# Batch 0's state softmax with tokens on partitions, in a fused cross-attention and PReLU MLP kernel on one core

## The chip, the cores and the metric

The kernel runs on one core of a Trainium2 chip. The metric is the time of one execution on the device, in microseconds (us). The engines are named as the profile names them: PE is TensorE (matrix products), PEld its weight load, DVE is VectorE, ACT is ScalarE, POOL is GpSimd and SP is SyncE. SBUF is the on-chip memory that the engines work in. PSUM is the memory into which PE writes: eight banks, each of 512 f32 values on each of 128 partitions.

## What is computed

Eight batches (B) of eight heads (H), each with 512 tokens (S) and 32 states (N) of width 64 (D). The 32 states of each head attend to the tokens and the tokens to the states; both reads are put side by side, and every row (4,352 of width 512) goes through an MLP with one hidden layer of 2,048 units and a PReLU with a slope for each unit.

```python
scores = scale * x @ state.T              # per batch and head: 512 x 32
a      = softmax(scores, over the 32 states)
xread  = a @ state
a2     = softmax(scale * state @ x.T, over the 512 tokens)
sread  = a2 @ x
rows   = concatenate([xread, sread], axis=2)    # 544 rows of 512 a batch
h   = rows @ w_in                          # 512 -> 2048
g   = maximum(h, 0) + alpha * minimum(h, 0)
out = g @ w_out                            # 2048 -> 512
```

## The kernel before

**The work.** For the token rows the kernel never makes xread. It multiplies the states of a batch by w_in first: `m = state @ w_in` (step `m.b.f`, L458, one for each batch and each quarter f of w_in, that is 512 hidden units; `mo`, L480, casts it to f16 into SBUF, in two halves of four heads). The first layer is then `h = a.T x m` (step `F.b.jc`, L491, for one of 16 blocks jc of 128 hidden units): two matmuls of 512 columns over the whole array, one for each half g of the heads. In batch 0 some of them are cut into their halves as steps `f.b.jc.g` (L512). Then ACT computes relu(-h) (step `N`, L523), DVE the PReLU from that and h (step `G`, L531), PE the second layer (step `S.b.q.jc2`, L543: two blocks jc for a quarter q of the tokens, over the whole array, 512 columns each), and `O` copies the result out of PSUM (L581) and issues its store. The state rows of all batches are a ninth batch at the end: `F.8` (L500), `R` (L591) and `RO`. The last quarter of the last batch is done in three pieces (`L`, L563, and `LO`, L574).

**Batch 0's way to its weights.** x is cast to f16 by its load (`lx0`, two halves by heads), turned by PE (`xt`, L288) and copied to SBUF (`xo`, L293; `xo2`, L296, is the same for batch 1). The states go the same way: `stc`, `stt`, `sto` for batch 0, whose load comes first; `str` (L234) and `sro` (L265, two copies of 896 columns) for the rest, whose load `lst` comes after the first x. Scores are computed by PE with the states on partitions (`sc`, L308: 64x32 tiles, eight for each half of the heads). The token softmax works on them as they are: `tm` (the maximum, L389, scaled at L392), `te` (exp with its sum, ACT, L400), `tsum` (L410), `tn` (POOL, L414), `tt` (a transposing DMA). The state softmax wants the 32 states of a token side by side. So DVE turns the scores in 32x32 blocks (`sb`, L343 for one half, L341 for a whole batch), takes the maximum over 32 columns (`smax`, L349), POOL subtracts it (`ssh.p`, L355), ACT takes exp (`sexp`, L361), DVE sums and inverts (`ssum`, L365 and L366), POOL scales to f16 (`snorm.p`, L369), and DVE turns the weights back in 32x32 blocks (`wb`, L377). Batch 0 does this in two halves of the heads, the later batches in one.

**What sets the order.** `ORDER` (L17 to L102) lists every step in the sequence in which each engine gets its instructions; nothing reorders them. A step's last arguments are its PSUM bank (k0 to k5) where it takes one, or its engine: a for ACT, v for DVE, p for POOL. A seventh tile of two banks, `two`, holds scores, or an `m` without a bank of its own. Each of these has one buffer, so the next user of a bank waits until the one before has been read. `Z.k.n` gives PE n x 128 columns of zeros to multiply (L218), to fill time in which nothing else is ready. The load of x of a batch (`lx`), of w_in by quarters (`wi`) and of w_out (`wo`) cast from f32 to f16 and are issued by POOL, in its instruction order, and run through one queue: `lx0.0 lx0.1 lst wi.0 lx.1 wi.1 wo.0 wi.2 wo.1 wi.3 wo.2 lx.2 wo.3`, then the other batches' x. From batch 2 on, x is turned by a DMA that SP issues (`xd`).

**Matmul shapes.** `sc` and `m` use 64x32 tiles of PE's array (the profile writes 64*32), the state reads `rd` (L433) 128*64; `xt`, `F`, `f`, `S` use the whole array (128*128). "Tiled" below means the former.

Of the kernel before, what the change touches and what calls it, by code (L numbers as in the profile page):

```python
# [34 lines left out]
S.0.0.7 S.0.3.6 N.1.1 G.1.1 N.1.3 tn.1.0 O.0.0.a te.2.0 F.1.5.4 S.0.3.7 N.1.5 G.1.3 F.1.9.2
S.1.1.0.5 G.1.7 F.1.4.3 smax.2 O.0.3.a S.1.1.1 tn.1.1 G.1.5 rd.0.0 te.2.1 N.1.9 G.1.9 m.2.3 F.1.6.1
N.1.4 rdo.0.a F.1.12.4 N.1.6 lx.3 G.1.4 F.1.13.0 N.1.12 F.1.8.2 G.1.6 G.1.12 S.1.2.0.3 N.1.13 G.1.13
ssh.p.2 N.1.8 S.1.1.2 F.1.11.1 G.1.8 F.1.10.4 N.1.11 S.1.2.1 N.1.10 G.1.11 G.1.10 S.1.2.2 sexp.2
S.1.1.3 ssum.2 F.1.14.0 F.1.15.2 snorm.p.2 mo.2.3.a.0 S.1.1.4 mo.2.3.a.1 S.1.1.5 m.3.2 m.4.2.1.4
N.1.14 tt.1 tsum.2 N.1.15 G.1.14 mo.3.2.a.1 S.1.1.6 S.1.2.3 S.1.2.4 mo.3.2.a.0 mo.4.2.a.0 G.1.15  # L40
# [612 lines left out]
```

## Time and profile before

| | us |
|---|---|
| median of 3 runs | 218.55 |
| lowest and highest run | 218.24, 218.85 |
| the profiled execution | 218.35 |
| its span, first to last instruction | 216.6 |
| PE busy in the span | 209.9 |
| DVE, ACT, POOL busy | 166.5, 137.2, 71.1 |

The profile is of one execution. A line of a group reads: source line, engine, operation, output <- inputs, tile of the array (rows*columns) where PE has one, output and input shapes (partitions x elements, type), count, then after the bar the busy time of all and the mean of one in ns, then the engine's idle time just before them and who ended it. A line of one instruction reads: start and length in us, engine, line, operation, and in brackets the wait before it and who ended it. "x8" behind such a line means that eight like it are put together, and the length covers them all. L12 is line 12 of the kernel.

### The profile page before, as it was taken

What the parts mean: (1) busy time and instruction counts of PE and PEld (TensorE: products, weight loads), DVE (VectorE), ACT (ScalarE), POOL (GpSimd) and SP (SyncE); (2) the same over time, 40 slices, a digit from 0 to 9 for tenths busy, and PEclk for the clock granted to TensorE, in tenths of its full rate; (3) what the DMA queues carried; (4) which work ended last, traced back from release to release, by engine and by line L of the source; (5) the groups of instructions that cost most, each with busy time, mean ns of one, the idle gap of its engine ahead of it and who ended that gap; (6) DMA issues with size and microseconds to landing.
All of it is one profiled execution on the core that took longest, in us unless ns stands there. A gap on an engine that the chain in (4) does not pass through costs nothing.

```text
span 216.6 us, 4193 instructions
## 1 busy us (share of the span) xinstructions
PE 209.9 (97%) x1637; PEld 99.9 (46%) x1637; DVE 166.5 (77%) x253; ACT 137.2 (63%) x271; POOL 71.1 (33%) x58
## 2 busy tenths in 40 slices
...
GB/s 89 174 196 206 207 199 183 127 206 127 59 137 145 81 213 98 51 108 195 174 109 97 100 50 49 2 97 48 53 147 24 28 48 48 48 47 4 48 100 145
DMA packets 39716, 23.12 MB, mean 107 GB/s; under 512 B 22144, under 2 KB 35984, under 8 KB 39696
## 3 DMA queue, kind: packets, MB, share of 16 engines
...
q14 instruction: 7, 0.06, 0.1%
...
## 4 chain that ended last, share of the span: by engine, by line
PE 90%; DMA 5%; POOL 2%; issue 1%; DVE 1%; ACT 0%; POOLq 0%
PE o L543 50%; PE h L491 25%; DMA w_in_sb<-in_moe_w_in_dram 5%; PE m_ps L458 4%; PE h L500 3%; PE o L591 3%; PE o L563 2%; PE sr_ps L433 2%; PE sc L308 1%; DVE m L480 1%; POOL xg L179 1%; POOL xg L162 0%; PE h L512 0%; POOL w_in_sb L198 0%; ACT m L480 0%
## 5 line engine op out<-in xcount | busy, mean ns | idle before, releaser
L543 PE MATMUL o<-w_out_sb,gt 128*128 128x512 f16 x496 | 125.3, 379 | 0.0
L523 ACT ACTIVATE neg<-h 128x512 f32<-128x512 f32 (+1 forms) x144 | 77.1, 579 | 46.8 <-PE h L491 37.4
L531 DVE SCALAR_TENSOR_TENSOR gt<-neg,oma_sb,h 128x512 f16<-128x512 f32 x128 | 89.9, 738 | 15.5 <-ACT neg L523 14.5
L543 PEld LDWEIGHTS <-gt 128*128 128x128 f16 x496 | 47.3, 98 | 55.3 <-issue 3.4
L491 PE MATMUL h<-aT,m 128*128 128x512 f16 x250 | 68.3, 379 | 0.0
L491 PEld LDWEIGHTS <-m 128*128 128x128 f16 x250 | 24.1, 98 | 28.3 <-issue 0.6
L414 POOL TENSOR_SCALAR e<-e,r 128x512 f16<-128x512 f16 x16 | 25.0, 1566 | 20.5 <-DVE r L410 16.6
L480 ACT CAST m<-m_ps 128x512 f16<-128x512 f32 x50 | 27.2, 611 | 4.5 <-PE m_ps L458 4.2
L369 POOL TENSOR_TENSOR an<-ts,r 128x1024 f16<-128x1024 f32 (+1 forms) x9 | 15.5, 1720 | 33.9 <-DVE r L366 14.8
L355 POOL TENSOR_TENSOR ts<-ts,mx 128x1024 f32<-128x1024 f32 (+1 forms) x9 | 15.5, 1721 | 28.7 <-DVE mx L349 28.7
L581 ACT COPY osb<-o 128x512 f32<-128x512 f32 x22 | 12.9, 591 | 14.9 <-PE o L543 14.9
L458 PE MATMUL m_ps<-w_in_sb,stT 64*32 64x512 f16 x256 | 11.4, 383 | 0.5 <-DMA w_in_sb<-in_moe_w_in_dram 0.4
L400 ACT ACTIVATE e<-sc,nb 128x512 f16<-128x512 f32 x16 | 11.2, 705 | 1.1 <-DVE nb L392 1.1
L377 DVE STREAM_TRANSPOSE aT<-an 128x1024 f16<-128x1024 f16 (+1 forms) x9 | 10.1, 1121 | 2.1 <-POOL an L369 2.1
L531 DVE SCALAR_TENSOR_TENSOR gs<-neg,oma_sb,h 128x256 f16<-128x256 f32 x16 | 7.5, 478 | 4.5 <-ACT neg L523 4.5
L480 DVE CAST m<-m_ps 128x512 f16<-128x512 f32 x14 | 9.1, 679 | 1.9 <-ACT m L480 1.6
L389 DVE TENSOR_REDUCE nb<-sc 128x2 f32<-128x1024 f32 x8 | 9.6, 1204 | 0.3 <-PE sc L308 0.3
L349 DVE TENSOR_REDUCE mx<-ts 128x32 f32<-128x1024 f32 (+1 forms) x9 | 9.8, 1091 | 0.0
L365 DVE TENSOR_REDUCE r<-ts 128x32 f32<-128x1024 f32 (+1 forms) x9 | 9.8, 1088 | 0.0
L500 PE MATMUL h<-XS,w_in_sb 128*128 128x256 f16 x64 | 9.4, 273 | 0.0
L601 DVE COPY osr<-o 128x512 f32<-128x512 f32 x1 | 0.7, 691 | 11.3 <-PE o L591 11.3
L361 ACT ACTIVATE ts<-ts 128x1024 f32<-128x1024 f32 (+1 forms) x9 | 8.7, 967 | 0.2 <-POOL ts L355 0.2
...
## 6 DMA issues: line engine op xcount, KB each, us to landing
...
```

The costliest lines, as they stand in the source:

```text
L355: engine(e).tensor_tensor(ts, ts, over_blocks(cols(live["mx", b], j, S // N)), ALU.subtract)
L369: engine(e).tensor_tensor(blocks(cols(live["an", b], j, S)), blocks(cols(live["ts", b], j, S)), over_blocks(cols(live["r1", b], j, S // N) ...
L400: nc.scalar.activation(live["e2", b][:, g, :, :], live["sc", b][:, :, :, g, :].rearrange("p r j s -> p (r j) s"), EXP, bias=live["nb", b][ ...
L414: nc.gpsimd.tensor_scalar_mul(e2, e2, live["r2", b][:, g : g + 1])
L458: nc.tensor.matmul(t[N * k : N * (k + 1), :], st_head(b, h)[64 * r : 64 * r + 64, :], w_in_sb[64 * r : 64 * r + 64, c, 512 * f : 512 * (f ...
L480: copier(e)(m_tile(b)[:, f, g, :], live["mp", b, f][g])
L491: nc.tensor.matmul(h.rearrange("p (r j s) -> p r j s", r=2, j=2), ms[b][:, f, g, 128 * j : 128 * (j + 1)], weights(b, g), start=(g == 0), ...
L500: nc.tensor.matmul(h, w_in_sb[:, c, 128 * jc : 128 * (jc + 1)], XS[:, c].rearrange("p q n b -> p (q n b)"), start=(c == 0), stop=(c == n_c ...
L523: nc.scalar.activation(neg, h, RELU, bias=0.0, scale=-1.0)
L531: nc.vector.scalar_tensor_tensor(gt, negs.pop((b, jc)), oma_sb[:, jc : jc + 1], h, ALU.mult, ALU.add)
L543: nc.tensor.matmul(outs[b, q], gts[b, jc][:, 128 * q : 128 * (q + 1)], w_out_sb[:, jc, :], start=(jc == 0), stop=(jc == n_jc - 1),)
L581: copier(e)(osb, t)
```

## The change

Batch 0's state softmax takes its scores in another form. The two halves g of the heads stay.

- `bdo.r` (`first_states_spread`) copies batch 0's states out of PSUM into `spread`, a zeroed tile in which each head has a 128 x 64 matrix: the head's states stand twice, once for the upper 64 rows and once for the lower. So `sto` leaves the PSUM tile alive.
- `tb.j.g` (`token_blocks`) multiplies turned x (128 tokens as weights) by that matrix: four whole-array matmuls of 64 columns, whose result has tokens on partitions and the 32 states of each token side by side. Both j of a half fill one bank.
- `bmax.g` takes the maximum and `bsh.g` subtracts it, on DVE, both straight from PSUM. They replace `sb.0`, `smax.0` and `ssh.p.0`.
- `sexp`, `ssum` and `snorm.p` are as before.
- `bt.g` (`first_weights_transposed`) turns the f16 weights back by four PE transposes into a bank, and `bto.g` copies them to SBUF. They replace `wb.0`.
- The scores with states on partitions are still computed once for the token softmax, as one `sc.0` instead of two halves.
- `zero` and a zero matmul's widest form are 384 columns instead of 512. The buffer `e2` has three copies instead of two.
- `ORDER` is new from end to end: sequence, banks and engines of the copies. `sro.0` and `xo` swap engines, for example, and batch 4's shift is `ssh.v.4` (DVE) where it was `ssh.p.4` (POOL). No other function is touched, and the steps of the other batches are the same list, in another sequence and with other banks and engines of copies.

```diff
 ORDER = """
-stc lx0.0 lx0.1 oma id Z.1.24 stt.0 Z.2.13 xt.0.0.0.1 sto.a xt.0.1.0.2 xo.0.0.0.v lst xo.0.1.0.v
-Z.0.6 sc.0.0 xt.0.1.1.3 xt.0.0.1.4 sb.0.0 xo.0.0.1.v smax.0.0 xo.0.1.1.a str.0.5 sc.0.1 str.1.0 wi.0
-sro.0.a lx.1 wi.1 ssh.p.0.0 sb.0.1 Z.1.3 sc.0 Z.5.7 m.0.0.1.2 sro.1.a sexp.0.0 smax.0.1 m.3.0.3.4
-ssh.p.0.1 tm.0 mo.0.0.a.1 sexp.0.1 ssum.0.0 m.1.0.5.0 ssum.0.1 te.0.1 te.0.0 mo.1.0.v.1 wo.0
-mo.1.0.a.0 snorm.p.0.0 mo.3.0.a.1 Z.2.23 xt.1.1.1.2 xt.1.0.1.2 xt.1.1.0.0 xt.1.0.0.0 mo.0.0.a.0
-snorm.p.0.1 wb.0.0 mo.3.0.a.0 m.2.0 f.0.0.0.5 f.0.1.0.4 wi.2 mo.2.0.a.0 wb.0.1 mo.2.0.a.1 f.0.1.1
-xo2.1.0.v N.0.1 m.0.1.1.3 f.0.0.1 mo.0.1.a.1 m.1.1 N.0.0 xo2.1.1.v mo.0.1.v.0 f.0.2.0.0 F.0.3.2
-f.0.2.1 F.0.4.1 mo.1.1.v.0 mo.1.1.a.1 F.0.7.3 G.0.1 N.0.2 G.0.0 wo.1 F.0.5.4 N.0.3 G.0.2 wi.3 m.4.0
-N.0.4 S.0.0.0.5 N.0.5 G.0.3 tsum.0 S.0.1.0.0 N.0.7 mo.4.0.a.1 G.0.4 S.0.0.1 S.0.1.1 G.0.5 mo.4.0.a.0
-tn.0.1 m.0.2.2.1 sc.1 G.0.7 S.0.2.0.4 mo.0.2.a.0 tm.1 m.1.2.2.3 wo.2 tn.0.0 mo.0.2.a.1 mo.1.2.a.0
-S.0.2.1 lx.2 wo.3 sb.1 F.0.6.1 F.0.9.2 mo.1.2.a.1 N.0.6 S.0.2.2 S.0.0.2 N.0.9 G.0.6 S.0.1.2 smax.1
-te.1.1 te.1.0 F.0.11.3 G.0.9 ssh.p.1 F.0.8.1 N.0.8 N.0.11 S.0.0.3 S.0.1.3 m.0.3 G.0.8 F.0.10.2
-mo.0.3.a.0 N.0.10 sexp.1 S.0.2.3 mo.0.3.v.1 xd.2 G.0.11 G.0.10 S.0.3.0.1 m.1.3 S.0.3.1 mo.1.3.a.0
-F.0.14.3 S.0.2.4 F.0.13.2 N.0.14 tt.0 ssum.1 S.0.0.4 S.0.1.4 S.0.0.5 S.0.3.2 G.0.14 F.0.12.3 N.0.13
-G.0.13 F.0.15.2 snorm.p.1 N.0.12 N.0.15 mo.1.3.a.1 wb.1 S.0.3.3 S.0.1.5 S.0.3.4 G.0.12 S.0.2.5
-G.0.15 S.0.3.5 F.1.2.3 S.0.2.6 N.1.2 F.1.0.2 tsum.1 S.0.2.7 N.1.0 S.0.1.6 S.0.1.7 G.1.2 O.0.2.a sc.2
...
-F.3.2.0 te.4.0 S.2.3.1 S.2.3.2 N.3.6 N.3.2 F.3.13.1 S.2.0.4 te.4.1 ssh.p.4 N.3.13 G.3.3 G.3.6
...
+stc lx0.0 lx0.1 id Z.1.24 stt.0 sto.a Z.2.13 xt.0.0.0.1 bdo.0.v oma xo.0.0.0.a xt.0.1.0.2 xo.0.1.0.a
+Z.5.9 xt.0.0.1.3 xt.0.1.1.4 lst xo.0.1.1.v bdo.1.a Z.1.4 tb.0.0.5 wi.0 xo.0.0.1.a tb.1.0.5 bmax.0
+tb.0.1.1 tb.1.1.1 bmax.1 str.1.2 bsh.0 str.0.0 lx.1 bsh.1 wi.1 Z.3.20 m.0.0.4.3 sro.1.a sro.0.v
+sexp.0.0 sc.0 sexp.0.1 mo.0.0.a.1 wo.0 m.3.0.5.2 ssum.0.0 mo.3.0.a.1 m.1.0.1.0 snorm.p.0.0
+mo.1.0.a.0 Z.3.10 m.4.0.3.2 mo.4.0.a.1 mo.0.0.a.0 mo.3.0.a.0 ssum.0.1 Z.1.10 bt.0.1 snorm.p.0.1
+Z.2.3 xt.1.1.1.2 xt.1.1.0.4 xt.1.0.0.4 mo.1.0.a.1 tm.0 bto.0.v mo.4.0.v.0 xt.1.0.1.2 te.0.0 bt.1.5
+f.0.2.0.1 bto.1.v f.0.0.0.0 f.0.1.0.3 xo2.1.0.v f.0.1.1 f.0.0.1 xo2.1.1.v m.0.1.5.4 te.0.1
+mo.0.1.v.1 f.0.2.1 N.0.1 N.0.0 mo.0.1.a.0 F.0.3.2 wi.2 G.0.1 G.0.0 m.1.1.4.5 N.0.2 G.0.2 mo.1.1.a.0
+m.2.0 F.0.4.3 N.0.3 mo.2.0.a.1 G.0.3 F.0.6.4 S.0.0.0.0 F.0.5.1 N.0.6 N.0.4 G.0.6 N.0.5 wo.1
+mo.2.0.a.0 S.0.2.0.2 mo.1.1.a.1 G.0.4 S.0.0.1 wi.3 S.0.2.1 m.0.2.4.3 mo.0.2.a.0 sc.1 G.0.5
+mo.0.2.a.1 tsum.0 sb.1 S.0.1.0.5 m.1.2.1.4 S.0.1.1 mo.1.2.a.1 F.0.7.3 tm.1 F.0.9.4 mo.1.2.a.0 N.0.7
+F.0.8.1 S.0.2.2 N.0.9 G.0.7 smax.1 G.0.9 te.1.1 te.1.0 N.0.8 S.0.0.2 F.0.11.3 N.0.11 wo.2 S.0.2.3
+S.0.1.2 lx.2 m.0.3 wo.3 G.0.8 F.0.10.4 tn.0.0 G.0.11 mo.0.3.a.1 S.0.0.3 ssh.p.1 S.0.1.3 mo.0.3.a.0
+N.0.10 F.0.14.1 m.1.3 sexp.1 F.0.12.3 G.0.10 S.0.2.4 ssum.1 S.0.0.4 S.0.1.4 S.0.2.5 F.0.13.4 N.0.12
+G.0.12 N.0.14 N.0.13 tn.0.1 S.0.0.5 G.0.14 S.0.3.0.3 tsum.1 S.0.3.1 snorm.p.1 F.0.15.1 S.0.1.5
+N.0.15 G.0.13 wb.1 G.0.15 S.0.3.2 S.0.3.3 xd.2 F.1.2.4 S.0.0.6 N.1.2 S.0.0.7 F.1.0.1 mo.1.3.a.1
+mo.1.3.a.0 tt.0 tn.1.1 S.0.1.6 G.1.2 O.0.0.v tn.1.0 S.0.2.6 N.1.0 G.1.0 m.2.1.4.0 sc.2 S.0.2.7
...
+G.3.8 ssh.v.4 F.3.9.5 G.3.7 N.3.4 N.3.9 F.3.0.2 sexp.4 S.2.0.5 S.2.3.0.3 G.3.4 S.2.0.6 tt.2 G.3.9
...
 """
@@ -207,18 +207,21 @@
         )
 
 
-    zero = consts.tile([128, 512], F16)
+    zero = consts.tile([128, 384], F16)
     nc.vector.memset(zero, 0.0)
 
     def zeros(k, n):
-        t = single(k, f"z_{len(zs)}", [128, 512], F32)
+        t = single(k, f"z_{len(zs)}", [128, 384], F32)
         zs.append(t)
         while n:
-            w = 128 * min(n, 4)
+            w = 128 * min(n, 3)
             nc.tensor.matmul(t[:, :w], zero[:, :128], zero[:, :w], start=True, stop=True)
             n -= w // 128
 
     zs = []
+
+    spread = consts.tile([128, H, 2, N], F16)
+    nc.vector.memset(spread, 0.0)
 
     oma_sb = consts.tile([128, n_jc], F32)
 
@@ -245,7 +248,7 @@
             twice_transposed(t[:, g, :], live["st0"][:, g, :])
 
     def first_states_out(e):
-        copier(e)(stT[:, :n0], live.pop("st0_ps").rearrange("d g p -> d (g p)"))
+        copier(e)(stT[:, :n0], live["st0_ps"].rearrange("d g p -> d (g p)"))
 
     def one_less_alpha():
         alT = consts.tile([128, 32], F32)
@@ -328,6 +331,60 @@
     def cols(t, j, n):
         return t if j is None else t[:, n * j : n * (j + 1)]
 
+    def first_states_spread(r, e):
+        d = slice(64 * r, 64 * r + 64)
+        copier(e)(
+            spread[d, :, r, :], live["st0_ps"][d].rearrange("d g (h n) -> d (g h) n", n=N)
+        )
+
+    def token_blocks(j, g, k):
+        if ("tp", g) not in live:
+            live["tp", g] = single(k, f"tp_{g}", [128, 2, 2, 4, N], F32)
+        for k in range(4):
+            h = 4 * g + (k ^ g)
+            nc.tensor.matmul(
+                live["tp", g][:, j, :, k, :],
+                live["xT", 0][:, h, j, :],
+                spread[:, h],
+                start=True,
+                stop=True,
+                skip_group_check=True,
+            )
+
+    def first_max(g):
+        if g == 0 or ("ts", 0) not in live:
+            halved.add(0)
+            live["ts", 0] = att.tile([128, 2 * S], F32, name="ts_0", tag="ts", bufs=2)
+            live["mx", 0] = att.tile([128, 2 * S // N], F32, name="mx_0", tag="mx", bufs=2)
+            live["r1", 0] = att.tile([128, 2 * S // N], F32, name="r1_0", tag="r1", bufs=2)
+            live["an", 0] = att.tile([128, 2 * S], F16, name="an_0", tag="an", bufs=2)
+            live["aT", 0] = att.tile([128, 2 * S], F16, name="aT_0", tag="aT", bufs=2)
+        nc.vector.tensor_reduce(
+            cols(live["mx", 0], g, S // N),
+            live["tp", g].rearrange("p j r k n -> p (j r k) n"),
+            AX.X, ALU.max,
+        )
+
+    def first_shift(g):
+        nc.vector.tensor_tensor(
+            blocks(cols(live["ts", 0], g, S)),
+            live.pop(("tp", g)).rearrange("p j r k n -> p (j r k) n"),
+            over_blocks(cols(live["mx", 0], g, S // N)),
+            ALU.subtract,
+        )
+
+    def first_weights_transposed(g, k):
+        t = live["wT", g] = single(k, f"wT_{g}", [128, 2, 2, 128], F16)
+        for j in range(2):
+            for r in range(2):
+                c = S * g + 256 * j + 128 * r
+                nc.tensor.transpose(t[:, r, j, :], live["an", 0][:, c : c + 128], ident)
+
+    def first_weights_out(g, e):
+        copier(e)(
+            cols(live["aT", 0], g, S), live.pop(("wT", g)).rearrange("p r j s -> p (r j s)")
+        )
+
     def score_blocks(b, j=None):
         if j in (None, 0):
             halved.discard(b) if j is None else halved.add(b)
@@ -394,7 +451,7 @@
     def token_exp(b, g):
         if ("e2", b) not in live:
             live["e2", b] = att.tile(
-                [128, 2, n_q, 128], F16, name=f"e2_{b}", tag="e2", bufs=2
+                [128, 2, n_q, 128], F16, name=f"e2_{b}", tag="e2", bufs=3
             )
             live["r2", b] = att.tile([128, 2], F32, name=f"r2_{b}", tag="r2", bufs=2)
         nc.scalar.activation(
@@ -607,7 +664,9 @@
         "lst": load_states, "wi": load_w_in, "wo": load_w_out, "lx": load_x,
         "stc": first_states_cast, "stt": first_states_transposed, "sto": first_states_out,
         "oma": one_less_alpha, "str": states_transposed, "sro": states_out,
-        "xd": x_transposed_dma, "xt": x_transposed, "xo": x_out, "xo2": x_out_both, "sc": scores,
+        "xd": x_transposed_dma, "xt": x_transposed, "xo": x_out, "xo2": x_out_both,
+        "bdo": first_states_spread, "tb": token_blocks, "bmax": first_max, "bsh": first_shift,
+        "bt": first_weights_transposed, "bto": first_weights_out, "sc": scores,
         "sb": score_blocks, "smax": state_max, "ssh": state_shift, "sexp": state_exp,
         "ssum": state_sum, "snorm": state_norm, "wb": weights_back,
         "tm": token_max, "te": token_exp, "tsum": token_sum, "tn": token_norm,
```

133 lines of the change are left out of this document (66 added, 67 removed).

## The prediction

> **What bounds the kernel now.** I read the page first, then the windows, then the chain in order of time. On the page TensorE (PE) is busy for 97% of the span and carries 90% of the chain; its matmuls overlap, so busy time alone doesn't prove that it is full.
>
> ```profile
> span 216.6 us, 4193 instructions
> PE 209.9 (97%) x1637; PEld 99.9 (46%) x1637; DVE 166.5 (77%) x253; ACT 137.2 (63%) x271; POOL 71.1 (33%) x58
> ...
> PE 90%; DMA 5%; POOL 2%; issue 1%; DVE 1%; ACT 0%; POOLq 0%
> ```
>
> The windows (length, then busy time of PE, PEld, DVE, ACT, POOL, then clock, DMA share and GB/s) say where PE is not full.
>
> ```profile
> 0.00:17.16 17.16, 13.81 (x153) 6.67 (x153) 11.20 (x26) 9.90 (x19) 11.75 (x20) 1.00 1.05 156
> 17.16:30.00 12.84, 12.75 (x110) 4.95 (x110) 12.22 (x19) 12.02 (x26) 8.19 (x7) 1.00 1.26 204
> 30.00:90.00 60.00, 59.83 (x531) 27.19 (x530) 55.22 (x78) 47.84 (x95) 23.61 (x15) 1.00 0.73 137
> 90.00:213.60 123.60, 123.56 (x848) 61.05 (x846) 87.91 (x133) 67.21 (x135) 27.56 (x17) 1.00 0.32 74
> ```
>
> From 17.16 us on PE misses 0.09, 0.17 and 0.04 us: it is full. Only the first 17.16 us, and how much work is left after them, can change. The chain (start, length) says what ends them, and gives the pace of a whole-array matmul of 512 columns, 2.16 / 10 = 0.216 us:
>
> ```profile
> 5.68 11.44 DMA w_in_sb<-in_moe_w_in_dram
> ...
> 84.84 2.16 PE o L543 x10
> ```
>
> The first row is the second quarter of w_in, issued at 5.68 and landed at 17.12. Step m.0.1 needs it, and hidden units 512 to 1023 need m.0.1. I call this **the gate**. PE just ahead of it and behind:
>
> ```profile
> 15.94 0.86 PE L512 MATMUL h<-aT,m 128*128 128x512 f16 x3
> 17.16 0.41 PE L458 MATMUL m_ps<-w_in_sb,stT 64*32 64x512 f16 x8 [0.36 <-DMA w_in_sb<-in_moe_w_in_dram]
> 17.50 0.39 PE L512 MATMUL h<-aT,m 128*128 128x512 f16 x1
> ```
>
> Three half first-layer products (step f) run from 15.94, then PE stands before the gate. The change cannot move the gate: its load has the same place in POOL's queue, behind the same five loads. It can only put more work ahead of it, and it must not delay what follows.
>
> **The state softmax, old and new.** Groups of the first 20 us (after the bar: busy us, mean ns of one), and two single rows:
>
> ```profile
> L355 POOL TENSOR_TENSOR ts<-ts,mx 128x512 f32<-128x512 f32 x2 | 2.1, 1050 | 3.8 <-DVE mx L349 3.8
> L265 ACT COPY stT<-st_ps 128x896 f16<-128x896 f16 x2 | 2.1, 1122 | 1.0 <-PE st_ps L234 1.0
> L369 POOL TENSOR_TENSOR an<-ts,r 128x512 f16<-128x512 f32 x2 | 2.1, 1039 | 0.5 <-DVE r L366 0.5
> L480 DVE CAST m<-m_ps 128x512 f16<-128x512 f32 x3 | 2.0, 671 | 0.1
> L343 DVE STREAM_TRANSPOSE ts<-sc 128x512 f32<-128x512 f32 x2 | 1.4, 718 | 0.9 <-PE sc L308 0.9
> L349 DVE TENSOR_REDUCE mx<-ts 128x16 f32<-128x512 f32 x2 | 1.4, 676 | 0.0
> L365 DVE TENSOR_REDUCE r<-ts 128x16 f32<-128x512 f32 x2 | 1.3, 654 | 0.0
> L296 DVE COPY xT<-xT_ps 128x1024 f16<-128x1024 f16 x2 | 1.2, 664 | 0.0
> L293 DVE COPY xT<-xT_ps 128x512 f16<-128x512 f16 x3 | 1.2, 412 | 2.3 <-PE xT_ps L288 2.3
> L389 DVE TENSOR_REDUCE nb<-sc 128x2 f32<-128x1024 f32 x1 | 1.2, 1215 | 0.0
> L366 DVE RECIPROCAL r<-r 128x16 f32<-128x16 f32 x2 | 0.5, 253 | 0.1
> ```
> ```profile
> 8.28 0.39 DVE L293 COPY xT<-xT_ps 128x512 f16<-128x512 f16 x1
> ...
> 14.13 1.32 PE L288 MATMUL xT_ps<-ident,xg 128*128 128x128 f16 x16
> ...
> 15.66 0.71 DVE L377 STREAM_TRANSPOSE aT<-an 128x512 f16<-128x512 f16 x1 [0.26 <-POOL an L369]
> ```
>
> Removed: four block transposes, 2 x 0.72 + 2 x 0.71 = 2.86 us of VectorE (DVE); both shifts on GpSimd (POOL), 2 x 1.05; sixteen small score matmuls. Added on PE, none of it in this trace: 16 score matmuls of 64 columns and 8 transposes of weights. The nearest row is the transposes of x, 16 in 1.32, so 24 take 2.0 us, between half of that (half the columns) and twice. They stand where zero matmuls fill time anyway, so PE pays nothing; the path pays some 0.3 us for each group. Added on DVE: two shifts out of PSUM (0.65, a reduction, to 1.05, POOL's; I take 0.70), a copy of 896 state columns from ACT (0.66 to 1.12; I take 1.0, as it reads strided, like ACT's), two copies of turned weights (0.41). ACT trades that copy (1.12) for two x copies and half a spread copy, under 0.6 each: +0.7 at most, under the 7.3 us that it idles in the first window. POOL's loads behind the gate are issued sooner, but the DMA share there is over 1, so none lands sooner. Batch 4's shift goes from POOL to DVE, with over 20 us between its scores and their use.
>
> Is it done before the gate? No scores stand ahead of the second x transposes now, and DVE does one x copy instead of three, so the copies are over by 8.2 us (8.67 before) and the first scores stand in PSUM at 8.4. From there DVE runs without a hole: two maxima 1.35, two shifts 1.40, state copy 1.00, two sums and reciprocals 1.81, token maximum and scaling 1.38, weights half 0 0.41, a cast 0.67, half 1 0.41: 8.43 us, to 16.8. In a full queue instructions overlap:
>
> ```profile
> 18.91 2.71 DVE L531 SCALAR_TENSOR_TENSOR gt<-neg,oma_sb,h 128x512 f16<-128x512 f32 x4
> 21.54 0.16 DVE L410 RECIPROCAL r<-r 128x2 f32<-128x2 f32 x1
> 21.61 0.73 DVE L531 SCALAR_TENSOR_TENSOR gt<-neg,oma_sb,h 128x512 f16<-128x512 f32 x1
> ```
>
> Four take 2.71 and one 0.73, so one per 0.66; with 0.06 saved by each of twelve it is 16.1. POOL's norms (1.04 each, from 13.1 at the latest) end by 15.2, off this path. The old half 1 was there at 15.66 + 0.71 = 16.37: **the state softmax itself gains next to nothing**. The old path waited for its engines in turn; the new one waits for DVE.
>
> **What it is worth.** The old order has three f steps behind m.0.1 (f.0.0.1 and both of jc 2), the new one has one. The two moved ahead fit into PE's hole before 17.12 and leave the full stretch: -0.43. Counting the orders, changes between tiled and whole-array matmuls behind m.0.1 fall from 41 to 40. One costs 0.10: m.0.1 takes 17.16 to 17.50 = 0.34, but three m steps in a row, the last matmul 0.39 long, pass at (0.86 - 0.39) / 2 = 0.235.
>
> ```profile
> 11.42 0.86 PE L458 MATMUL m_ps<-w_in_sb,stT 64*32 64x512 f16 x24
> ```
>
> All else behind m.0.1 is the same list in another sequence. So -0.53 if no wait changes.
>
> **New waits**, PSUM bank by bank behind the gate. PE: m.0.1 to 17.50, f and F.0.3 to 18.15, change to 18.25. There m.1.1 wants bank 4, which holds half of m.0.1 (done 17.57) until DVE's cast ends at 18.3: +0.08. m.1.1, m.2.0 and a change end at 18.9; F.0.4 wants bank 3, free after prelu G.0.1, 18.25 + 0.73 = 18.98: +0.1. F.0.4, F.0.6, S.0.0.0, F.0.5 take PE to 20.73; S.0.2.0 wants bank 2, free after the fourth prelu at 18.25 + 2.71 = 20.96: +0.23. All of PE is queued behind them; nothing makes it up. Together +0.41, and I add 0.15 for batch 1's weights, whose way from scores to use shrinks from 14.1 to 13.2 us of PE work. **Old waits** that may go:
>
> ```profile
> 22.59 0.41 PE L458 MATMUL m_ps<-w_in_sb,stT 64*32 64x512 f16 x8
> 23.09 0.41 PE L308 MATMUL sc<-xT,stT 64*32 64x256 f16 x16
> ...
> 88.83 0.40 PE L308 MATMUL sc<-xT,stT 64*32 64x256 f16 x16
> 89.37 0.41 PE L458 MATMUL m_ps<-w_in_sb,stT 64*32 64x512 f16 x8
> ```
>
> 0.50 instead of 0.235 ahead of batch 1's scores: 0.26 lost, which the new order doesn't repeat (m.2.0, whose bank they want, is cast earlier). 0.54 instead of about 0.24 at 88.83: 0.3, which may come back elsewhere. Sum: -0.53 + 0.41 + 0.15 - 0.26 = **-0.2**. The tail ends in the same last copy and store. The profiled execution took 218.35 (span 216.6 and 1.75 around it), so 218.1 by it; the median is 218.55, so I forecast 218.3. About 0.3% (0.65 us) is what a measurement can tell from no change.
>
> **Rivals.**
> *Waits vanish.* Both old waits go and the new ones don't come (shifts at 0.65, prelus from 17.9): 218.55 - 0.53 - 0.56 + 0.1 = 217.6. For it: the old order lost almost nothing after 17.16. Against: the three bank waits are written into the new one. 0.18.
> *DVE late at the gate.* Shifts at 1.05, copy at 1.12 and no overlap: half 1 at 17.6, m.0.1 half a microsecond late, and the change doesn't do what it says, as other DVE work fills the place of the block transposes: 218.8. For it: the sum above has 0.3 to spare. 0.11.
> *Banks too tight (slower).*
>
> ```profile
> L523 ACT ACTIVATE neg<-h 128x512 f32<-128x512 f32 (+1 forms) x144 | 77.1, 579 | 46.8 <-PE h L491 37.4
> ...
> L491 PE MATMUL h<-aT,m 128*128 128x512 f16 x250 | 68.3, 379 | 0.0
> ```
>
> A bank is free again 0.16 (379 less 216) + 0.58 + 0.73 us after its first-layer product, with three handings-over of some 0.05: 1.6. The old order returns to such a bank within 2 us four times, the new one thirteen times, mostly after 1.73. It decides where a prelu starts over 0.1 late. About one DVE instruction in three is one of 1.2 us, so four of thirteen might meet one, by 0.6 each: 2.4 us in a blind order, none in the old one's four; I take 1.0: 219.3. For it: DVE is busy 55.2 of 60. 0.27.
> *Half clock.* The same matmul, twice:
>
> ```profile
> 1.31 2.74 PE L218 MATMUL z<-zero 128*128 128x512 f16 x6 [1.31 <-DVE zero L211]
> ...
> 12.61 1.40 PE L218 MATMUL z<-zero 128*128 128x512 f16 x6 [0.34 <-ACT m L480]
> ```
>
> Six in 2.74, then six in 1.40; the granted clock reads 1.00 in both, so only the spacing tells. Between 14.1 and 17.1 the new PE does 24 transposes, five f and few zeros. If that slowed it again for the length of the start (1.3 to 6.6), half of 5.3 us is lost: 218.3 + 2.6 = 220.9. Against: 16 transposes and three f stood there before, at full pace. 0.04. The Trainium skill, "TensorE: Matmul & The Clock Gate", Part 4, says that transposes don't count as work for the gate that halves the clock, and Part 1 that an idle window of about 3.4 us closes it; this rival is what that rule would do. The full pace behind the 16 transposes of before neither confirms nor refutes it.
>
> **How the numbers follow.** Forecast 218.3: 0.40. Faster is the first rival, 0.18; same is forecast and second rival, 0.51; slower is banks and clock, 0.31. The range goes from 217.6 to 219.5 and leaves out the clock and the far half of the banks.
>
> **What would show it.** Right: m.0.1 still at 17.16 with five f ahead of it; state weights copied by 16.8; waits near 18.3, 18.9 and 20.8; S.0.0.0 near 19.9. Wrong: f steps behind m.0.1 beyond one, or PE windows after 30 us that miss over 0.5 us (banks), or whole matmuls at 0.43 after 14 us. A w_in landing at another time than 17.1 would upset all of it.

## The result and the profile after

The changed kernel takes 218.26 us (median of 22 runs, 217.56 to 218.90) and the kernel before 218.53 (22 runs, 218.09 to 218.96). The ratio is 0.9981, with a 95% interval of 0.9973 to 0.9990: 0.42 us less. (The ratio isn't formed from the two medians, which are 0.27 us apart.) The interval leaves out 1, so the gain is clear of noise, but it is inside what the prediction called the same (0.3%). The profiled execution took 217.94, its span is 216.2.

The page after: span, busy time of PE, and the chain's shares by engine.

```profile
span 216.2 us, 4232 instructions
PE 210.0 (97%) x1658; PEld 101.1 (47%) x1658; DVE 165.2 (76%) x253; ACT 139.3 (64%) x275; POOL 67.0 (31%) x55
...
PE 93%; DMA 3%; POOL 1%; issue 1%; ACT 0%; POOLq 0%
```

The same four windows as before (length, then busy time of PE, PEld, DVE, ACT, POOL):

```profile
0.00:17.16 17.16, 13.98 (x174) 8.26 (x175) 10.65 (x26) 10.59 (x20) 10.62 (x19) 1.00 1.05 156
17.16:30.00 12.84, 12.83 (x110) 4.96 (x109) 12.64 (x19) 12.67 (x29) 5.63 (x6) 1.00 1.26 205
30.00:90.00 60.00, 60.00 (x532) 27.05 (x532) 57.63 (x83) 47.09 (x92) 24.03 (x16) 1.00 0.73 137
90.00:213.60 123.60, 123.16 (x846) 60.81 (x844) 84.28 (x127) 68.98 (x138) 26.67 (x16) 1.00 0.30 75
```

The reader sees two things. From 17.16 to 90 us PE misses 0.01 us by this view, 0.26 before (tiled groups that run long count as busy; the account below has them); the last window is only the earlier end. And between 17.16 and 30 us DVE and ACT are now full too: 12.64 and 12.67 of 12.84.

The timeline of PE around the gate and behind it:

```profile
13.49 0.41 PE L515 MATMUL m_ps<-w_in_sb,stT 64*32 64x512 f16 x8
13.83 0.72 PE L218 MATMUL z<-zero 128*128 128x384 f16 x4
14.61 0.38 PE L381 MATMUL wT<-ident,an 128*128 128x128 f16 x4
14.83 0.33 PE L218 MATMUL z<-zero 128*128 128x384 f16 x1
15.21 1.05 PE L291 MATMUL xT_ps<-ident,xg 128*128 128x128 f16 x16
16.10 0.39 PE L381 MATMUL wT<-ident,an 128*128 128x128 f16 x4
16.32 1.27 PE L569 MATMUL h<-aT,m 128*128 128x512 f16 x5
17.52 0.47 PE L515 MATMUL m_ps<-w_in_sb,stT 64*32 64x512 f16 x8
17.93 0.39 PE L569 MATMUL h<-aT,m 128*128 128x512 f16 x1
18.19 0.59 PE L548 MATMUL h<-aT,m 128*128 128x512 f16 x2
18.79 0.85 PE L515 MATMUL m_ps<-w_in_sb,stT 64*32 64x512 f16 x16
19.57 1.04 PE L548 MATMUL h<-aT,m 128*128 128x512 f16 x4
...
20.88 0.59 PE L548 MATMUL h<-aT,m 128*128 128x512 f16 x2
21.42 1.46 PE L600 MATMUL o<-w_out_sb,gt 128*128 128x512 f16 x6
22.81 0.52 PE L515 MATMUL m_ps<-w_in_sb,stT 64*32 64x512 f16 x8
23.04 0.51 PE L311 MATMUL sc<-xT,stT 64*32 64x256 f16 x16
23.48 0.61 PE L600 MATMUL o<-w_out_sb,gt 128*128 128x512 f16 x2
```

Five f steps stand ahead of m.0.1, as forecast, but m.0.1 starts at 17.52, 0.36 later than before. PE did not stand before it this time: the fifth f starts at 17.22 in the trace, and 0.216 and one shape change of 0.09 behind that is 17.52. The load landed at 17.41. So PE's own work and the load end together here.

The old wait at 88.83, between batch 5's scores and m, is gone. The same place after:

```profile
89.08 0.63 PE L515 MATMUL m_ps<-w_in_sb,stT 64*32 64x512 f16 x16
89.53 0.40 PE L311 MATMUL sc<-xT,stT 64*32 64x256 f16 x16
89.86 1.90 PE L600 MATMUL o<-w_out_sb,gt 128*128 128x512 f16 x8
```

The account from both traces, against the prediction's terms (us; tiled steps are held against their length where nothing waits, 0.34 for one m with the change behind it, 0.56 for two; a wait is named by the start of the matmul ahead of it):

| term | forecast | measured | where it is read |
|---|---|---|---|
| start of m.0.1 | 0 | +0.36 | 17.16, then 17.52 |
| two f steps ahead of it | -0.43 | -0.43 | three f ahead, then five |
| shape changes | -0.10 | -0.10 | one fewer in the trace |
| waits of the new order | +0.56 | +0.64 | m.0.1 0.06; before F.0.3 0.05; before m.1.1 0.08; m.1.1 and m.2.0 take 0.78 instead of 0.56; before S.0.2.0 0.11; m and sc.1 0.67 instead of 0.56 |
| waits of the old order gone | -0.26 | -0.81 | 0.28 ahead of sc.1, 0.30 at 88.8, 0.11 at 30.2, 0.12 at 93.4 and 95.2 |
| not assigned | | -0.06 | |
| sum | -0.2 | -0.40 | spans 216.6 and 216.2 |

The total came near the forecast by luck: m.0.1 0.36 later, which the prediction had ruled out, is outweighed by 0.55 us of old waits that it hadn't counted on.

The two traces can also be cut at the start of m.0.2, from where on PE has the same matmuls left in both. That is at 22.59 before and 22.81 after, so up to there the changed kernel is 0.22 us *behind*; from there to the end of the span it takes 193.36 us instead of 193.98. In these two executions the whole gain lies behind the part in which batch 0's softmax stands, in waits of the old order that the new one doesn't have.

One thing about the code, for reading the experiments: the kernel before computes batch 0's scores with states on partitions twice, in two halves for the state softmax and once more (`sc.0`) for the token softmax. The change drops the halves and keeps `sc.0`.

### The profile page after: what moved, and what is told of

Read it like the earlier page. It is cut to its first block, busy times and chain, and to the rows that moved or that the text cites. A ratio compares the mean times of both kernels' runs of the same rounds, so it can differ in the third digit from the quotient of the medians.

```text
span 216.2 us, 4232 instructions
## 1 busy us (share of the span) xinstructions
PE 210.0 (97%) x1658; PEld 101.1 (47%) x1658; DVE 165.2 (76%) x253; ACT 139.3 (64%) x275; POOL 67.0 (31%) x55
## 4 chain that ended last, share of the span: by engine, by line
PE 93%; DMA 3%; POOL 1%; issue 1%; ACT 0%; POOLq 0%
PE o L600 50%; PE h L548 25%; PE m_ps L515 4%; DMA w_in_sb<-in_moe_w_in_dram 3%; PE h L557 3%; PE o L648 3%; PE sr_ps L490 2%; PE o L620 2%; PE sc L311 1%; PE z L218 1%; PE h L569 1%; POOL xg L179 1%; PE xT_ps L291 0%; PE wT L381 0%; ACT m L537 0%
## 5 line engine op out<-in xcount | busy, mean ns | idle before, releaser
L580 ACT ACTIVATE neg<-h 128x512 f32<-128x512 f32 (+1 forms) x144 | 78.1, 580 | 43.6 <-PE h L548 37.4
L548 PEld LDWEIGHTS <-m 128*128 128x128 f16 x250 | 23.9, 98 | 28.4 <-issue 1.0
L537 ACT CAST m<-m_ps 128x512 f16<-128x512 f32 x54 | 29.6, 603 | 7.5 <-PE m_ps L515 7.3
L412 POOL TENSOR_TENSOR ts<-ts,mx 128x1024 f32<-128x1024 f32 x6 | 11.5, 1913 | 25.6 <-DVE mx L406 25.6
L638 ACT COPY osb<-o 128x512 f32<-128x512 f32 x19 | 11.3, 594 | 4.5 <-PE o L600 4.5
L162 POOL DMA_DIRECT2D xg<-in_x_dram x7 | 6.5, 934 | 12.9 <-PE sr_ps L490 12.9
L638 DVE COPY osb<-o 128x512 f32<-128x512 f32 x12 | 8.1, 680 | 1.3 <-PE o L600 1.3
L218 PE MATMUL z<-zero 128*128 128x384 f16 (+2 forms) x34 | 7.7, 359 | 1.3 <-DVE zero L211 1.2
L434 DVE STREAM_TRANSPOSE aT<-an 128x1024 f16<-128x1024 f16 x7 | 8.7, 1238 | 0.2
```

The lines of the kernel that those rows point to most:

```text
L412: engine(e).tensor_tensor(ts, ts, over_blocks(cols(live["mx", b], j, S // N)), ALU.subtract)
L537: copier(e)(m_tile(b)[:, f, g, :], live["mp", b, f][g])
L548: nc.tensor.matmul(h.rearrange("p (r j s) -> p r j s", r=2, j=2), ms[b][:, f, g, 128 * j : 128 * (j + 1)], weights(b, g), start=(g == 0), ...
L580: nc.scalar.activation(neg, h, RELU, bias=0.0, scale=-1.0)
L638: copier(e)(osb, t)
```

## The experiments

"Fillers" are the steps Z. Ratios are to the kernel before on the same chip; "landing" is where w_in's second quarter lands in the run's trace.

**Fewer zeros.** Two fillers out of the changed kernel.

```diff
-... mo.3.0.a.0 ssum.0.1 Z.1.10 bt.0.1 snorm.p.0.1
-Z.2.3 xt.1.1.1.2 xt.1.1.0.4 ...
+... mo.3.0.a.0 ssum.0.1 bt.0.1 snorm.p.0.1
+xt.1.1.1.2 xt.1.1.0.4 ...
```

> The changed kernel without two fillers of zeros (0.72 and 0.33 us of TensorE, at 13.8 and 14.8 us), nothing else. In the changed kernel m.0.1 starts at 17.52, 0.37 later than before; its load landed at 17.41 there (17.11 before), and TensorE came from a full stretch that began at 13.49. Theory A (TensorE itself was late, since fillers hold up the transposes): the five f steps end by 16.9, TensorE waits for the load, and m.0.1 starts within 0.1 us of the landing; 0.1 us less than the changed kernel if the load lands at 17.4, 0.4 less if at 17.1. Theory B (the load sets it, and lands later because of the changed order): m.0.1 at 17.5 with TensorE idle before it, and no gain. Theory C (half clock): matmuls of 512 columns 0.43 us apart behind 14 us, and 1 to 3 us more.

Measured: 217.79 us, 0.9963 (0.9951 to 0.9975).

```profile
15.82 1.27 PE L569 MATMUL h<-aT,m 128*128 128x512 f16 x5
17.54 0.41 PE L515 MATMUL m_ps<-w_in_sb,stT 64*32 64x512 f16 x8 [0.44 <-DMA w_in_sb<-in_moe_w_in_dram]
```

The five f are through 0.5 us earlier and PE waits for the load, which landed at 17.50 here: theory A. Behind it little is gained. S.0.2.0 starts at 21.42 as in the changed kernel, when DVE's fourth prelu of this row ends (21.37 in both):

```profile
18.66 4.88 DVE L588 SCALAR_TENSOR_TENSOR gt<-neg,oma_sb,h 128x512 f16<-128x512 f32 x7
```

(the changed kernel's row; the first prelu starts at 18.66 in both). A second time:

> Fewer zeros again, for a second trace and a narrower interval: so far 0.9963 (0.9951 to 0.9975) of before, the changed kernel 0.9981 (0.9973 to 0.9990) and, again, 0.9960 (0.9945 to 0.9976). Theory A (without fillers m.0.1 starts when its load lands): m.0.1 within 0.15 us of the landing and TensorE's five f steps ended before it; ratio 0.995 to 0.9975, so below the 0.9981. Theory B (fillers cost nothing where batch 1's x lands late, as it did at 15.14 us in the second trace of the changed kernel): ratio 0.9965 to 0.9985, no different from the changed kernel.

Measured: 217.89 us, 0.9980 (0.9964 to 0.9997). This load landed at 16.73:

```profile
15.64 1.27 PE L569 MATMUL h<-aT,m 128*128 128x512 f16 x5
16.84 0.47 PE L515 MATMUL m_ps<-w_in_sb,stT 64*32 64x512 f16 x8
...
18.11 1.03 PE L515 MATMUL m_ps<-w_in_sb,stT 64*32 64x512 f16 x16
...
22.19 0.62 PE L515 MATMUL m_ps<-w_in_sb,stT 64*32 64x512 f16 x8
22.43 0.60 PE L311 MATMUL sc<-xT,stT 64*32 64x256 f16 x16
```

Without the fillers m.0.1 is right behind the load: 17.54 behind 17.50, 16.84 behind 16.73. In the second execution PE's own work ended no sooner: the fifth f starts at 16.53, and 0.216 and 0.09 behind that is 16.84. Of the 0.70 that this execution is ahead at m.0.1, only 0.4 is left in the span (216.1 and 215.7): m.1.1 and m.2.0 take 0.96 instead of 0.66, m and sc.1 0.77 instead of 0.56. As to the time, the two measurements don't settle whether fewer zeros beats the changed kernel.

**The changed kernel again.**

> The changed kernel unaltered, beside the other two and for a second trace. Theory A (where loads land differs from execution to execution by some tenths, and m.0.1 starts at the later of the landing and the end of TensorE's own work, about 17.5): m.0.1 between 17.4 and 17.9 wherever the load lands, the waits of 0.2 to 0.3 us near 22.6, 30.2 and 88.9 not there, ratio to before 0.997 to 0.999. Theory B (the landing at 17.41 belongs to the changed order): it lands at 17.3 to 17.5 again, m.0.1 within 0.1 us of it.

Measured: 217.66 us, 0.9960 (0.9945 to 0.9976), a little under the first result's interval. So the same kernel gave ratios 0.2% apart in two measurements, and smaller differences between measurements decide nothing. Theory A's ratio was missed. The load landed at 17.40 and m.0.1 started at 17.52, both as in the first trace, so this run alone doesn't part the theories; a landing fixed by the changed order (B) doesn't fit the 16.73 above. The old waits aren't there. What PE waited for was another load: batch 1's x, issued at 4.83, landed 10.3 us later, at 15.14, and its transposes started at 15.19. In the first trace it landed at 14.30 and the transposes stood behind fillers until 15.21. So by these two traces fillers cost something only in executions where that x is early.

**The old form in the new order.** Batch 0's softmax as before the change, at the places of the new one; the shifts go to GpSimd behind the loads it has to issue (other places for them weren't tried).

```diff
-... bdo.1.a Z.1.4 tb.0.0.5 wi.0 xo.0.0.1.a tb.1.0.5 bmax.0
-tb.0.1.1 tb.1.1.1 bmax.1 str.1.2 bsh.0 str.0.0 lx.1 bsh.1 wi.1 ...
+... Z.1.4 wi.0 xo.0.0.1.a sc.0.0 sb.0.0 smax.0.0
+sc.0.1 sb.0.1 smax.0.1 str.1.2 str.0.0 lx.1 wi.1 ssh.p.0.0 ssh.p.0.1 ...
...
-bt.0.1 ... bto.0.v ... bt.1.5 ... bto.1.v
+... wb.0.0 ... wb.0.1
```

> The changed kernel's order from end to end, with batch 0's state softmax in the old form (scores with states on partitions, block transposes on VectorE, shifts on GpSimd) at the places of the new one. Theory A (the gain lies in the order, not in the form): weights of half 1 ready by 16.9 as in the changed kernel, five f steps ahead of m.0.1, m.0.1 between 17.2 and 17.6, and a time within 0.2 us of the changed kernel (ratio to before 0.997 to 0.999). Theory B (the new form is what makes room ahead of the gate): weights of half 1 after 17.4, m.0.1 at 17.9 or later, a time at or over that of before, 218.5 to 219.

Measured: 218.54 us, 1.0003 (0.9992 to 1.0013). m.0.1 starts at 18.04 with its load landed at 16.95: theory B. The profile says through which engine. ACT in this kernel, and then in the changed one:

```profile
11.24 0.62 ACT L418 ACTIVATE ts<-ts 128x512 f32<-128x512 f32 x1
12.55 0.63 ACT L418 ACTIVATE ts<-ts 128x512 f32<-128x512 f32 x1 [0.68 <-POOL ts L412]
13.08 1.54 ACT L537 CAST m<-m_ps 128x512 f16<-128x512 f32 x3
```
```profile
10.71 1.14 ACT L418 ACTIVATE ts<-ts 128x512 f32<-128x512 f32 x2
12.10 1.56 ACT L537 CAST m<-m_ps 128x512 f16<-128x512 f32 x3 [0.25 <-PE m_ps L515]
```

The second exp waits 0.68 for POOL's shift, and the casts of m are queued behind it: 13.08 instead of 12.10. Some 0.5 of that is a later x (it landed at 7.41, 6.93 in the changed kernel). PE's next m, the transposes of x and the f steps follow the casts.

**The old form, fewer zeros.** Both edits above.

```diff
-... Z.1.10 bt.0.1 ... Z.2.3 ...
+... (the old form as above, without these two fillers)
```

> The changed order with the old form of the state softmax and without the two fillers. Theory A (the form itself is worth next to nothing; with the fillers in place the old form was 0.3 us slower than the new one because exp of half 1 came 0.7 us later on ScalarE, so the casts, the fillers behind them and the transposes of x came later): m.0.1 at 17.3 to 17.7, 217.8 to 218.2, within 0.3 of fewer zeros with the new form. Theory B (the new form is what makes room ahead of the gate): m.0.1 stays near 18.0, and 218.4 to 218.7.

Measured: 218.62 us, 0.9997 (0.9985 to 1.0010). My theory A fell, theory B holds: m.0.1 started at 18.27, its load landed at 17.41. Fillers aren't in the way here, the casts are (and batch 0's x landed late again, at 7.66):

```profile
15.21 2.05 ACT L537 CAST m<-m_ps 128x512 f16<-128x512 f32 x4 [0.34 <-PE m_ps L515]
...
15.85 1.32 PE L291 MATMUL xT_ps<-ident,xg 128*128 128x128 f16 x16 [0.73 <-ACT m L537]
```

**The new form in the old order.** The new steps at the places of the old ones. Banks for the turned weights were found by letting 1 and 5 change roles from the first f on.

```diff
-... sc.0.0 ... sb.0.0 ... smax.0.0 ... sc.0.1 ... ssh.p.0.0 sb.0.1 ... smax.0.1 ... ssh.p.0.1
+... tb.0.0.1 tb.1.0.1 ... bmax.0 ... bsh.0 ... tb.0.1.2 tb.1.1.2 ... bmax.1 bsh.1
-wb.0.0 mo.3.0.a.0 m.2.0 f.0.0.0.5 f.0.1.0.4 wi.2 mo.2.0.a.0 wb.0.1
+bt.0.4 bto.0.v mo.3.0.a.0 m.2.0 bt.1.5 f.0.0.0.1 f.0.1.0.4 wi.2 mo.2.0.a.0 bto.1.v
```

> The order of the kernel before with the new form of batch 0's state softmax in the places of the old one (for the banks of the turned weights, banks 1 and 5 change roles from the first f on). Theory A (what bounds that order is the load of w_in and the f steps behind it, not the softmax): m.0.1 within 0.1 us of the landing, three f steps ahead of it, 218.3 to 218.7, the same as before. Theory B (the new form saves time by itself): 217.9 to 218.2.

Measured: 218.84 us, 1.0014 (0.9995 to 1.0034): no gain. m.0.1 starts at 17.72, 0.3 behind the landing at 17.38: theory A's 0.1 is missed, in the direction away from theory B. The old order's waits are there:

```profile
23.85 0.41 PE L311 MATMUL sc<-xT,stT 64*32 64x256 f16 x16 [0.25 <-ACT m L537]
...
89.58 0.40 PE L311 MATMUL sc<-xT,stT 64*32 64x256 f16 x16
90.12 0.41 PE L515 MATMUL m_ps<-w_in_sb,stT 64*32 64x512 f16 x8
```

So neither half of the change gains by itself: the new form alone 1.0014, the new order alone 1.0003, both 0.9981. Cut at m.0.2, the traces say where. From there to the end the old order takes 193.98 us and, with the new form, 194.13; the new order takes 193.36 and, with the old form, 193.46. So the new order keeps its gain there with the old form too, and loses it ahead: m.0.2 starts 6.6 us behind the landing of w_in's second quarter with the old form in the new order (some 0.5 of it the later x), 5.4 in the changed kernel, 5.5 before.

**Heads and tails exchanged.** First the changed order up to m.2.0, then what is left in the old order:

```diff
 ... G.0.1 G.0.0 m.1.1.4.5 N.0.2 G.0.2 mo.1.1.a.0 m.2.0
-F.0.4.3 N.0.3 mo.2.0.a.1 G.0.3 F.0.6.4 S.0.0.0.0 F.0.5.1 ...
+mo.2.0.a.0 mo.2.0.a.1 F.0.4.1 mo.1.1.a.1 F.0.7.3 wo.1 F.0.5.4 N.0.3 wi.3 N.0.4 S.0.0.0.5 ...
```

> The changed kernel's order up to F.0.3 and m.2.0 (18.9 us), and from there the steps that are left in the order of the kernel before. Theory A (the head's gain of 0.53 us is eaten by m.0.1, 0.37 later, and the rest of the gain is three waits of the old order that are gone, 0.69 us in all): the waits near 22.6, 30.2 and 88.9 come back, at least 0.4 us of them, and the time is 218.3 to 218.8, not faster than before by over 0.1%. Theory B (the head carries the gain): 217.9 to 218.2, as fast as the changed kernel or faster.

Measured: 219.31 us, 1.0040 (1.0028 to 1.0052). Then the old order up to F.0.3, and what is left in the changed one:

```diff
 ... mo.0.1.v.0 f.0.2.0.0
-F.0.3.2 f.0.2.1 F.0.4.1 mo.1.1.v.0 mo.1.1.a.1 F.0.7.3 G.0.1 ...
+m.4.0.3.2 mo.4.0.a.1 mo.4.0.v.0 f.0.2.1 F.0.3.2 G.0.1 G.0.0 N.0.2 G.0.2 mo.1.1.a.0 F.0.4.3 ...
```

> The order and softmax of the kernel before up to F.0.3 (18.4 us), then the steps that are left in the changed kernel's order (with three buffers for e2, as there). Theory A (the gain is waits of the old order that are gone behind 22 us): m.0.1 at 17.16, none of the waits of 0.1 to 0.3 us at 22.6, 30.2 and 88.9, and 217.9 to 218.3, 0.2 to 0.6 less than before. Theory B (the head carries the gain): 218.4 to 218.8.

Measured: 219.12 us, 1.0032 (1.0020 to 1.0044). Both are slower than either whole order, and both by waits at the joint, which neither theory had. PE in the first, then in the second:

```profile
21.20 1.46 PE L548 MATMUL h<-aT,m 128*128 128x512 f16 x6 [1.12 <-DVE gt L588]
```
```profile
19.37 1.46 PE L491 MATMUL h<-aT,m 128*128 128x512 f16 x6 [0.41 <-ACT m L480]
21.39 0.59 PE L543 MATMUL o<-w_out_sb,gt 128*128 128x512 f16 x2 [0.57 <-DVE gt L531]
```

As times they decide nothing. Their traces still show to which order the later waits belong: the waits near 30.2 and 88.8 are in the first (there at 31.6 and 90.4) and not in the second. The wait ahead of sc.1 is in neither.

**m.2.0 ahead of the gate.**

```diff
-... m.0.1.5.4 te.0.1 ... mo.1.1.a.0
-m.2.0 F.0.4.3 ...
+... te.0.1 m.2.0 m.0.1.5.4 ... mo.1.1.a.0
+F.0.4.3 ...
```

(with the edit of fewer zeros)

> The changed kernel without the two fillers (as in the first run of fewer zeros, 217.8), and with m.2.0 moved from behind m.1.1 to just ahead of m.0.1 (te.0.1 ahead of it, since m.2.0 takes the two banks that it reads). In fewer zeros TensorE stood idle from 16.9 to 17.5 ahead of m.0.1. Theory A (TensorE has slack ahead of the gate now and is full behind it): m.2.0 fits into that hole, 0.2 to 0.3 us less behind it, 217.5 to 217.7. Theory B (behind the gate VectorE and ScalarE, 12.6 of 12.8 us busy, set the pace and not TensorE): the time stays at 217.7 to 217.9 and the waits near 18.3 and 21 us grow by what m.2.0 leaves.

Measured: 218.03 us, 0.9968 (0.9955 to 0.9981): no gain over fewer zeros, theory B. The load landed at 17.11. Batch 1's x landed at 14.96, so the five f ended only just ahead of m.2.0 and this execution had no hole to fill: m.2.0 started at 17.33, m.0.1 itself at about 17.56, where fewer zeros had it behind a later landing. What m.2.0 left behind the gate became wait: 0.30 instead of 0.10 ahead of F.0.4, for DVE's first prelu. And the wait of 0.23 ahead of S.0.2.0 stands at 20.98 in both traces; DVE's fourth prelu ends it, at 21.37 in both.

**Three f ahead instead of five** (with the edit of fewer zeros).

```diff
-f.0.2.0.1 bto.1.v f.0.0.0.0 f.0.1.0.3 xo2.1.0.v f.0.1.1 f.0.0.1 xo2.1.1.v m.0.1.5.4 te.0.1
-mo.0.1.v.1 f.0.2.1 ...
+bto.1.v f.0.0.0.0 f.0.1.0.3 xo2.1.0.v f.0.1.1 xo2.1.1.v m.0.1.5.4 te.0.1
+mo.0.1.v.1 f.0.0.1 f.0.2.0.1 f.0.2.1 ...
```

> Fewer zeros (217.8) with three f steps ahead of m.0.1, as in the kernel before, instead of five: f.0.2.0 and f.0.0.1 stand behind it. Theory A (a step moved ahead of the gate is worth its 0.216 us behind it): 0.43 us more, 218.1 to 218.3. Theory B (behind the gate TensorE waits for VectorE anyway, so that two more steps fill waits): the waits at 18.3 and 21 us shrink by 0.2 to 0.4, and 217.7 to 217.95.

Measured: 218.08 us, 0.9985 (0.9974 to 0.9997). Against the first measurement of fewer zeros that is 0.22% or 0.48 us more, about the two f steps; against the second it is 0.1 us. As a time it leaves both theories open. The trace leans to theory B: with its load at 17.06 m.0.1 started at 17.10, 0.44 earlier than in the first trace of fewer zeros, the two more f stand where that one waited, and S.0.2.0 starts at 21.46 instead of 21.42.

**No zeros behind 9 us.** All four fillers out.

```diff
-... lx.1 bsh.1 wi.1 Z.3.20 m.0.0.4.3 ... mo.1.0.a.0 Z.3.10 m.4.0.3.2 ... Z.1.10 bt.0.1 ... Z.2.3 xt.1.1.1.2 ...
+... lx.1 bsh.1 wi.1 m.0.0.4.3 ... mo.1.0.a.0 m.4.0.3.2 ... bt.0.1 ... xt.1.1.1.2 ...
```

> The changed kernel without any of the four fillers behind 9 us (1.26, 0.70, 0.72 and 0.33 us). Theory A (fillers are only in the way): m.0.1 within 0.1 us of the landing, whole-array matmuls of 512 columns 0.216 us apart behind 16 us, 217.6 to 218.0 as in fewer zeros. Theory B (half clock: TensorE stands idle for much of 9 to 14 us, and its clock falls): matmuls 0.43 us apart behind 14 us for up to 5 us, and 218.5 to 221.

Measured: 218.19 us, 0.9978 (0.9969 to 0.9987).

```profile
13.77 0.40 PE L381 MATMUL wT<-ident,an 128*128 128x128 f16 x4 [0.48 <-POOL an L426]
14.39 1.07 PE L291 MATMUL xT_ps<-ident,xg 128*128 128x128 f16 x16 [0.23 <-DMA xg<-in_x_dram]
15.30 0.39 PE L381 MATMUL wT<-ident,an 128*128 128x128 f16 x4
15.52 1.27 PE L569 MATMUL h<-aT,m 128*128 128x512 f16 x5
18.14 0.41 PE L515 MATMUL m_ps<-w_in_sb,stT 64*32 64x512 f16 x8 [1.35 <-DMA w_in_sb<-in_moe_w_in_dram]
```

Five matmuls of 512 columns in 1.27, the last 0.38 long, are 0.22 apart: full pace, behind 24 transposes and with no filler. Theory A holds, and m.0.1 is 0.04 behind its load, which landed at 18.10, the latest of all. The time is above the 218.0 that theory A allowed, but the kernel before took 218.71 on this chip and 218.47 on the one that gave 217.8; 0.9978 of that is 218.0.

**The gate moved.** The load of w_in's second quarter ahead of batch 1's x, which then is turned behind the f steps (with the edit of fewer zeros; from F.0.7 on, banks 2 and 4 are exchanged).

```diff
-... str.0.0 lx.1 bsh.1 wi.1 ...
+... str.0.0 wi.1 bsh.1 lx.1 ...
-... f.0.1.1 f.0.0.1 xo2.1.1.v m.0.1.5.4 te.0.1 mo.0.1.v.1 f.0.2.1 ... F.0.3.2 ... m.1.1.4.5 ... m.2.0 F.0.4.3 ...
+... f.0.1.1 f.0.0.1 m.0.1 N.0.1 mo.0.1.v.1 f.0.2.1 ... F.0.3.4 G.0.1 wi.2 xt.1.1.1.5 xt.1.0.1.5 xt.1.1.0.0 xt.1.0.0.0
+N.0.2 G.0.0 F.0.4.3 N.0.3 m.2.0 xo2.1.0.v G.0.2 F.0.6.2 ... xo2.1.1.v S.0.2.1 m.1.1 ... sc.1 ...
```

> Fewer zeros with the load of w_in's second quarter ahead of batch 1's x in POOL's queue, so that it should land near 14.3 us instead of 16.9 to 18.1. m.0.1 goes ahead of the f steps' neighbours, batch 1's x is turned and copied behind them, m.1.1 comes later, banks 2 and 4 change roles. Theory A (the gate is what holds TensorE in the first 18 us): no wait for w_in's second quarter, and 217.0 to 217.6, up to 0.8 us less than fewer zeros (217.8). Theory B (without the gate VectorE is the bound at once: eight prelus of 0.66, two copies of x of 0.66 and the casts stand behind the weights): TensorE waits for banks between 18 and 22 us instead, and 217.7 to 218.5.

Measured: 219.63 us, 1.0058 (1.0042 to 1.0074). Theory A fell, and theory B was too mild. The load landed at 14.38 and nothing waited for it:

```profile
14.84 1.52 PE L569 MATMUL h<-aT,m 128*128 128x512 f16 x5
...
17.29 1.06 PE L291 MATMUL xT_ps<-ident,xg 128*128 128x128 f16 x16
18.34 0.59 PE L548 MATMUL h<-aT,m 128*128 128x512 f16 x2
...
24.81 0.41 PE L311 MATMUL sc<-xT,stT 64*32 64x256 f16 x16 [0.50 <-ACT m L537]
```

By 18.34 PE has done what the first trace of fewer zeros had done by about 18.5. Behind that stand waits of 0.2 to 0.6 us at 18.9, 19.6, 20.2, 20.9, 23.9, 25.6 and 27.7. The trace names ACT's casts of m, DVE's prelus and once its copy of x at their ends; the one quoted is for m.1.1, which this edit puts just ahead of sc.1. So the place of m.1.1 is a fault of this order, and how much of the loss the moved gate itself has isn't separated.

## Why the prediction was right, and where it wasn't

**Right in the total and in the sign, by luck in where it came from:** 218.3 forecast, 218.26 measured. Up to m.0.2 the prediction's terms make the changed kernel earlier, and it was 0.22 us later; the old waits behind that made up for it. By steps:

**"The change cannot move the gate", m.0.1 at 17.16: wrong.** It started at 17.52. Two things were missed. PE's added work was costed at nothing, because zero matmuls fill that time anyway. But in this order the fillers stand ahead of the transposes of x and the five f steps, and from 13.49 on PE had no slack left: 0.72 and 0.33 of fillers, 1.05 of x transposes, two groups of turned weights, five f. Fewer zeros shows it: the same steps end 0.5 earlier. And the landing isn't a constant: with the same five loads ahead of it, it was at 16.73 to 18.10 in the thirteen traces that have that order, 17.11 in the one that I took it from. A rival isn't ruled out: with the shifts gone from GpSimd, w_out's first load is issued at 6.42 instead of 12.28, behind w_in's. In the four traces where it is issued late w_in landed at 16.86 to 17.41, in the nine where it is issued early at 16.73 to 18.10.

**Weights of half 1 by 16.1 to 16.8: 0.15 late.** The copy ran from 16.52 to 16.95. The copies of x were over at 8.06 (8.2 forecast), two maxima took 1.29 and two shifts 1.28 (forecast 1.35 and 1.40), both out of PSUM:

```profile
8.09 1.29 DVE L362 TENSOR_REDUCE mx<-tp 128x16 f32<-128x512 f32 x2
9.30 1.28 DVE L369 TENSOR_TENSOR ts<-tp,mx 128x512 f32<-128x512 f32 x2
...
16.52 0.42 DVE L384 COPY aT<-wT 128x512 f16<-128x512 f16 x1 [0.47 <-PE wT L381]
```

The last row's wait names the cause: PE, not DVE, was late with half 1. The Trainium skill, "VectorE: DVE Perf Modes", under "Why PSUM operands drop a tier", has f32 operands in PSUM at the lowest rate. The maximum out of SBUF took 0.676 before, two out of PSUM take 1.29 here, so no run here shows a loss by it.

**"The state softmax itself gains next to nothing": true of the old order, not of the new one.** In the old order the new form gave 1.0014. In the new order it is what separates 0.9981 from 1.0003. I looked at DVE's sum; in the traces the mechanism is in ACT's queue, where the second exp no longer waits for POOL and the casts come earlier.

**Two f steps and one shape change, -0.53: as forecast** by the count of matmuls in the trace. But S.0.2.0, which DVE's fourth prelu releases, starts at 21.42 to 21.46 in the changed kernel, in the first trace of fewer zeros and with three f ahead. So it may be that two f behind the gate would only have stood in the new waits, and that this term and the next are largely one; no pair of runs separates them.

**New waits, +0.56: measured +0.64,** partly at other places. The first came as named, for DVE's cast of m.0.1 (0.08 at 18.41). The second, for prelu G.0.1, didn't: PE had already lost 0.22 at m.1.1's other half, waiting for ACT's cast of m.0.1. The third came, for the fourth prelu, with 0.11 instead of 0.23 (at 21.10). In the first trace of fewer zeros all three are there, with 0.16, 0.10 and 0.23. Batch 1's weights cost nothing; the 0.11 at sc.1 is another wait, for a prelu.

**Old waits, -0.26: measured -0.81.** The wait at 88.83 was left out as one that "may come back elsewhere", and the 0.11 at 30.2 and 0.12 near 94 weren't counted. None came back. Every trace with the old tail has them, none with the new one.

**The rivals.** *Banks too tight* didn't happen in the whole new order: PE is busy 60.00 of 60 us from 30 to 90, though by the prediction's count thirteen banks are taken again within 2 us. Its mechanism is real where an order isn't matched to DVE, as at the joints and with the gate moved. *Half clock* is refuted for this start by the kernel without zeros: behind its transposes, 13.77 to 15.52 with nothing else on PE, the five f are 0.22 apart. The Trainium skill, "TensorE: Matmul & The Clock Gate", has transposes not count as work for the gate (Part 4) and an idle window of some 3.4 us close it (Part 1). Those 1.75 us are shorter than that window, so no run here tests the rule. *Waits vanish* came for the old waits and not for the new ones.

Still open: whether fewer zeros is faster than the changed kernel (0.9963 and 0.9980 against 0.9981 and 0.9960), what the two f steps ahead of the gate are worth, and why landings spread.
